# Half of the heads by 128 tokens, scores a pair ahead, loads behind points of TensorE's work

## The chip, the cores and the metric

The kernel runs on one core of a Trainium2 chip. The metric is device time in microseconds (us) of one execution; the median of several runs is given. Engines: PE is TensorE (matmul), PEld its weight loads, DVE is VectorE, ACT is ScalarE, POOL is GpSimd, SP the queue that issues all loads and stores here.

## The reference

The first part is attention with exponential decay, by blocks of 64 tokens. Shapes: q, k, v (4 batches, 8 heads, 768 tokens, 64 channels), float32, one decay `lam` for each head.

```python
for b in range(nb):                       # 12 blocks of 64 tokens
    intra = (qb @ kb.T) * Dmask           # Dmask[i, j] = lam**(i - j) for i >= j, else 0
    out_b = intra @ vb + (qb * lam**(pos + 1)) @ kv_state
    kv_state = lam**64 * kv_state + (kb * lam**(63 - pos)).T @ vb
```

The block length is a matter of arithmetic only: a state carried by 128 tokens, with a mask of 128 x 128, gives the same output. Then `x` (3072 tokens, 512 features) goes through a soft mixture of 8 experts with 4 slots each:

```python
logits = x @ phi                                  # (3072, 32)
d = softmax over tokens (axis 0); c = softmax over the 32 slots (axis 1)
slot_input = d.T @ x                              # 32 slots x 512
slot_out = relu(slot_input @ w1[e]) @ w2[e]       # w1, w2: 2 MB for each expert
y = c @ slot_out                                  # (3072, 512)
```

## The kernel before

Heads are taken in pairs: 64 channels of one head on partitions 0 to 63, of the other on 64 to 127, so there are four head pairs (`hp`), and `hh` is the half. Tokens come in chunks of 128. `PAIR[p]` takes the same chunk of two batches (index `x`); twelve pairs `p` run through the attention loop. On `s` runs the half of a chunk, 64 tokens.

One pass of the loop `for p in range(NP)`, in order on TensorE: `scores` (64x64 products of k and q into banks w0, w1; VectorE multiplies by the decay mask into `at`), `turn_k` (transposes of k; VectorE scales into `kd`), `turn_x` (transposes of the chunk finished a pass ago; ScalarE copies into `x`), `logits` in even passes or `slots` in odd ones for the group of two pairs before, `values` for the products of the other half-head's rows, `state` (kd with v, for both halves of 64 tokens), `values` again, and `carried` (the state with q scaled by `scale_q` on GpSimd) for both halves. `advance` takes the state from one half to the next: VectorE adds, GpSimd multiplies by lam**64. `evict` copies the result from four banks to `xt` on ScalarE. The two rounds of `values` differ in whether the row half and the bank half agree; the second waits for a small ScalarE copy behind the first (`behind`, `token`). Odd passes also run the softmax over slots of one group (`slot_softmax`).

Each engine keeps the order in which the program is written (`InOrder`). A float32 matmul call shows as two matmul records and two weight loads in the trace, a transpose as one of each.

All loads go through SP, in program order. At the top of pass p it has q, k, v of pair p + 2 (512 KB each, two buffers each) and up to four slabs of w1 (512 KB each, 32 slabs in all): `EARLY[p]` says how many. SP sends off whatever has a free buffer, so a load waits only for the reader of its buffer.

After the loop (the tail): the last group's logits and weights, the slot inputs, layer one (`first`, w1), layer two (`second`, w2, loaded into freed buffers: six of q, k, v, three of the work tiles, then slabs as layer one frees them), the softmax over slots transposed and stacked (`parts`, `CR`, `CT`), and the output product and stores (`put`), two chunks at a time.

Of the kernel before, what the change touches and what calls it, by code (L numbers as in the profile page):

```python
# [8 lines left out]
F32 = mybir.dt.float32  # L9
# [24 lines left out]
EARLY = (4, 3, 3, 3, 3, 3, 3, 3, 3, 3)  # L34
# [17 lines left out]
def decay_attn_soft_moe(  # L52
# [40 lines left out]
    def load_in(p, which):  # L93
        for x in which:
            tl = loads.tile([P, 2, 512], F32, tag=x, name=x)
            b, n = PAIR[p]
            src = {"q": qT, "k": kT, "v": vN}[x].rearrange("(b n) p c -> n p b c", n=NB)
            sp.dma_start(out=tl, in_=src[n, :, b:b + 2])
            IN[x, p] = tl

# [11 lines left out]
    def load_early(n):  # L112
        for _ in range(n):
            Q, kc, q = early.pop()
            t_ = slabs.tile([P, 2, 512], F32, tag="slab", name="w1t")
            sp.dma_start(out=t_, in_=w1[4 * Q + q, kc])
            wt["w1", Q, q, kc] = t_

    def load_late(pool_=None, tag="slab", bufs=None):
# [3 lines left out]
        sp.dma_start(out=t_, in_=w2[4 * Q + 2 * i:4 * Q + 2 * i + 2, f].rearrange("e p d -> p e d"))  # L123
        for y in range(2):
            wt["w2", Q, 2 * i + y, f] = t_[:, y, :]

# [10 lines left out]
    load_early(1)  # L137
# [4 lines left out]
    wps = bank("s0")  # L142
# [12 lines left out]
    mask = work.tile([P, 2, HP, C], F32, tag="mask", name="mask")  # L155
    for hh in range(2):
        for hp in range(HP):
            y = hh * HP + hp
            dve.tensor_tensor_scan(
                out=mask[:, hh, hp, :],  # L160
                data0=lam_sb[:, y:y + 1].broadcast_to([P, C]),
                data1=ident2,
                initial=0.0,
                op0=ALU.mult,
                op1=ALU.add,
            )
    kpow = mask.rearrange("p a b i -> p b a i")[:, :, :, C - 1:C].broadcast_to([P, HP, 2, DH])

    qpow = work.tile([P, HP, C], F32, tag="qpow", name="qpow")
    lam64 = qpow.rearrange("p (o a) i -> p o a i", o=1)[:, :, :, C - 1:C].broadcast_to([P, 2, HP, DH])  # L170

    def powers():
        for hp in range(HP):
            dve.tensor_tensor_scan(
                out=qpow[:, hp, :],
                data0=lam_sb[:, 8 + hp:9 + hp].broadcast_to([P, C]),
                data1=zero.broadcast_to([P, C]),
# [3 lines left out]
            )  # L181

    CN = const.tile([P, T, SL], F32, name="CN")
    acc = const.tile([P, D], F32, name="acc")
    lsum = const.tile([P, 1], F32, name="lsum")
    e = const.tile([P, P], F32, name="e")
    d = const.tile([P, P], F32, name="d")
    L = const.tile([P, P], F32, name="L")


    AT, KD, QS, ST, DEC, XT, X = {}, {}, {}, {}, {}, {}, {}
    run = {}

    def scores(p):
        k_, q_ = (IN[x, p].rearrange("p x (a s i) -> p x a s i", a=HP, s=2) for x in "kq")
        sc = [bank("w0"), bank("w1")]
        for x in range(2):
            for hp in range(HP):
                c = slice(x * 256 + hp * C, x * 256 + hp * C + C)
                for s in range(2):  # L200
                    for hh in range(2):
                        r = slice(C * hh, C * hh + C)
                        pe.matmul(
                            out=sc[hh][C * s:C * s + C, c],
                            lhsT=k_[r, x, hp, s],
                            rhs=q_[r, x, hp, s],
# [3 lines left out]
        at = work.tile([P, 2, 2, HP * C], F32, tag="at", name="at")  # L210
        for hh in range(2):
            m = mask[:, hh].rearrange("p (o a) i -> p o (a i)", o=1).broadcast_to([P, 2, HP * C])
            dve.tensor_tensor(out=at[:, hh], in0=sc[hh].rearrange("p (x c) -> p x c", x=2), in1=m, op=ALU.mult)
        AT[p] = at.rearrange("p b x (a i) -> p b x a i", a=HP)

    def scale_q(p):
        n = PAIR[p][1]
        qs = work.tile([P, 2, HP, 2, C], F32, tag="qs", name="qs")
        for x in range(2):
            q_ = IN["q", p][:, x].rearrange("p (a s i) -> p a s i", a=HP, s=2)  # L220
            s = slice(0 if n else 1, 2)
            m = qpow.rearrange("p a (o i) -> p a o i", o=1).broadcast_to([P, HP, 2, C])
            pool.tensor_tensor(out=qs[:, x, :, s], in0=q_[:, :, s], in1=m[:, :, s], op=ALU.mult)
        QS[p] = qs

    def turn_k(p):
        kd = work.tile([P, 2, HP, 2, DH], F32, tag="kd", name="kd")
        for x in range(2):
            tk = bank(f"t{x}")
            for hp in range(HP):  # L230
                c = slice(hp * P, hp * P + P)
                pe.transpose(tk[:, c], IN["k", p][:, x, c], ident)
            dve.tensor_tensor(
                out=kd[:, x], in0=tk.rearrange("p (a b c) -> p a b c", a=HP, b=2), in1=kpow, op=ALU.mult
            )
        KD[p] = kd

    def turn_x(p, tags):
        for x in range(2):
            t = chunk(p, x)  # L240
            tr = bank(tags[x])
            for y in range(HP):
                pe.transpose(tr[:, y * P:y * P + P], XT[t][:, y, :], ident)
            xn = keep.tile([P, D], F32, tag="x", name="x", bufs=6)
            act.copy(out=xn, in_=tr)
            X[t] = xn

    KV = {}

    def state(p):  # L250
        halves = (0, 1) if PAIR[p][1] < NB - 1 else (0,)
        kv = [bank(f"s{s}") for s in halves]
        v_, kd = IN["v", p].rearrange("p x (h c) -> p x h c", h=H), KD.pop(p)
        for x in range(2):
            for hp in range(HP):
                c = slice(x * 256 + hp * C, x * 256 + hp * C + C)
                for hh in range(2):
                    for s in halves:
                        r = slice(C * s, C * s + C)
                        pe.matmul(  # L260
                            out=kv[s][C * hh:C * hh + C, c],
                            lhsT=kd[r, x, hp, hh],
                            rhs=v_[r, x, HP * hh + hp],
                            start=True,
                            stop=True,
                        )
        for s in halves:
            KV[p, s] = kv[s].rearrange("p (x a c) -> p x a c", x=2, a=HP)

    def advance(p, s):  # L270

        if (p, s) not in KV:
            return
        kv = KV.pop((p, s))
        st = work.tile([P, 2, HP, DH], F32, tag="st", name="st", bufs=2)
        if PAIR[p][1] == 0 and s == 0:
            dve.tensor_copy(out=st, in_=kv)
        else:
            dve.tensor_tensor(out=st, in0=DEC.pop("d"), in1=kv, op=ALU.add)
        ST[p, s] = st  # L280
        if s == 0 and PAIR[p][1] == NB - 1:
            return
        dec = work.tile([P, 2, HP, DH], F32, tag="dec", name="dec")
        pool.tensor_tensor(out=dec, in0=st, in1=lam64, op=ALU.mult)
        DEC["d"] = dec

    def place(xb, x, hh, hp, s):
        g, a = divmod(hp, 2)
        return xb[x][hh][C * a:C * a + C, g * P + C * s:g * P + C * s + C]

    token = head.tile([P, 1], F32, name="token")

    def behind(ins, earlier):
        how = mybir.DependencyInfo(mybir.DependencyClass.Sync, mybir.DependencyReason.DATA)
        tc.add_manual_dep(ins.ins, earlier.ins.name, how, reason="row tiles change banks")
        return ins

    def values(p, xb, same):
        v_, at = IN["v", p].rearrange("p x (h c) -> p x h c", h=H), AT[p]
        for x in range(2):  # L300
            for g in range(2):
                for a in range(2):
                    for s in range(2):
                        hh, hp = s if same else 1 - s, 2 * g + a
                        r = slice(C * s, C * s + C)
                        mm = pe.matmul(
                            out=place(xb, x, hh, hp, s),
                            lhsT=v_[r, x, HP * hh + hp],
                            rhs=at[r, hh, x, hp],
                            start=(not same and g == 0),  # L310
                            stop=True,
                            skip_group_check=True,
                        )
                        if same and x + g + a + s == 0:
                            behind(mm, run["crossed"])
        if not same:

            run["crossed"] = behind(act.copy(out=token, in_=zero), mm)

    def carried(p, s, xb):  # L320
# [430 lines left out]
```

## Time and profile before

| What | Value |
|---|---|
| median of three runs | 205.86 us (205.21 to 208.71) |
| the profiled execution | 207.05 us, span 205.3 us |
| attention, first scores to last logits | 5.87 to 147.61 us |
| tail, to the end of the span | 57.66 us |
| granted TensorE clock, mean over the span | 0.902 |
| moved by DMA | 59.35 MB, mean 289 GB/s |
| loads and stores of 512 KB (256 KB for the output) | 100 (24) |

Span is from the first to the last instruction of the profiled execution; some time lies around it. A busy TensorE isn't TensorE at its peak, since matmuls overlap and their ends are modelled: the work of a group is better read from the distance between starts. "Issue" as a releaser means that an engine waited for nothing that the profile shows. Granted clock 1.00 is 2.4 GHz, 0.50 is 1.2 GHz.

### The profile page before, as it was taken

To read this page: it belongs to the slowest core of one execution; us is meant where nothing else is said; L and a number is where in the kernel's file an instruction comes from. 1 tells how busy PE (TensorE), PEld (TensorE's weight loads), DVE (VectorE), ACT (ScalarE), POOL (GpSimd) and SP (SyncE) were. 2 spreads that over 40 slices of the span, in tenths; PEclk is the share of its full clock that TensorE was granted. 3 is DMA by queue.
4 is the path that set the end of the run, shared out by engine and by line. 5 is a ranking of instruction groups with operands and counts; after the bars stand their busy time and mean duration, and the time that the engine had idled before them with its cause. 6 is when DMAs were issued, how large, how long until landed. Compare 5 with 4: busy or idle time off the path is not lost. (4 is left out here: it accounts for less than half of the span.)

```text
span 205.3 us, 8546 instructions
## 1 busy us (share of the span) xinstructions
PE 149.8 (73%) x3850; PEld 113.6 (55%) x3850; DVE 95.4 (46%) x198; ACT 56.9 (28%) x162; POOL 57.0 (28%) x72
## 2 busy tenths in 40 slices
PE   7496398397575997398295974768969999998800
PEld 7385297376565795387284854656833335444700
DVE  2835143063851663553535443755510779543800
ACT  2013022124023232224022122233320179441700
POOL 1236260262622420442602612444000049000000
PEclk9969958789996799979759699999999999999995
DMA  6999976479887299788759298445677999999996
GB/s 196 372 397 413 410 284 228 187 220 346 260 321 300 44 316 381 295 214 328 286 163 374 82 306 313 161 154 174 162 286 266 364 374 407 404 408 387 383 384 214
DMA packets 30389, 59.35 MB, mean 289 GB/s; under 512 B 2704, under 2 KB 8848, under 8 KB 30352
## 3 DMA queue, kind: packets, MB, share of 16 engines
q1 hardware_dynamic: 30352, 58.80, 80.5%
q8 instruction: 30, 0.49, 0.9%
q14 instruction: 7, 0.06, 0.1%
HBM read 52.50 MB, written 6.29 MB: 286 GB/s over the span
## 5 line engine op out<-in xcount | busy, mean ns | idle before, releaser
L46 POOL TENSOR_TENSOR dec<-st,qpow 128x512 f32<-128x512 f32 x20 | 21.2, 1059 | 75.5 <-DVE st L46 75.5
L46 DVE TENSOR_TENSOR st<-dec,s 128x512 f32<-128x512 f32 x20 | 13.7, 686 | 46.5 <-PE s L46 28.9
L46 POOL TENSOR_TENSOR qs<-q,qpow 128x512 f32<-128x512 f32 (+1 forms) x24 | 28.1, 1192 | 14.7 <-DVE qpow L46 7.9
L46 PE MATMUL t<-at,v 64*64 64x64 f32 x768 | 19.6, 231 | 15.2 <-issue 8.6
L46 PE MATMUL t<-qs,st 64*64 64x64 f32 x704 | 18.0, 247 | 14.3 <-issue 14.3
L46 PEld LDWEIGHTS t<-at,v 64*64 64x64 f32 x768 | 15.6, 141 | 22.2 <-issue 10.0
L46 PE MATMUL w<-q,k 64*64 64x64 f32 x768 | 19.2, 254 | 8.7 <-issue 7.2
L46 PEld LDWEIGHTS t<-qs,st 64*64 64x64 f32 x704 | 15.8, 158 | 15.5 <-issue 15.2
L46 ACT COPY xt<-t 128x256 f32<-128x256 f32 x48 | 14.5, 387 | 33.8 <-PE t L46 33.8
L46 DVE TENSOR_TENSOR at<-w,mask 128x512 f32<-128x512 f32 x24 | 15.4, 685 | 16.5 <-PE w L46 16.4
L46 PEld LDWEIGHTS w<-q,k 64*64 64x64 f32 x768 | 17.5, 167 | 9.8 <-issue 8.5
L46 ACT COPY x<-t 128x512 f32<-128x512 f32 x24 | 12.9, 584 | 20.6 <-PE t L46 20.6
L46 PE MATMUL w<-w2t,hz 128*32 128x256 f32 (+1 forms) x224 | 17.2, 414 | 0.9 <-DMA w2t<-w_x 0.9
L46 PE MATMUL t<-ident,k 128*128 128x128 f32 x96 | 16.5, 328 | 0.0
L46 DVE TENSOR_TENSOR kd<-t,mask 128x512 f32<-128x512 f32 x24 | 15.7, 683 | 0.8 <-PE t L46 0.7
L46 PE MATMUL t<-w1t,e 128*32 128x512 f32 x128 | 14.1, 594 | 0.4 <-DVE e L46 0.4
L46 PEld LDWEIGHTS t<-ident,k 128*128 128x128 f32 x96 | 14.0, 173 | 0.6
L46 PE MATMUL t<-ident,xt 128*128 128x128 f32 x96 | 14.0, 294 | 0.0
L46 PE MATMUL s<-v,kd 64*64 64x64 f32 x704 | 13.8, 221 | 0.0
L46 PEld LDWEIGHTS s<-v,kd 64*64 64x64 f32 x704 | 12.7, 138 | 0.0
L46 PEld LDWEIGHTS t<-ident,xt 128*128 128x128 f32 x96 | 12.5, 156 | 0.2 <-issue 0.2
L46 PEld LDWEIGHTS w<-w2t,hz 128*32 128x32 f32 x224 | 6.7, 109 | 9.3 <-issue 3.7
(105 smaller groups left out, 157.8 us busy)
## 6 DMA issues: line engine op xcount, KB each, us to landing
w1t<-w_x SPq DMA_DIRECT2D x32, 512.0 KB, 6.8
w2t<-w_x SPq DMA_DIRECT2D x32, 512.0 KB, 6.8
k<-kT SPq DMA_DIRECT2D x12, 512.0 KB, 3.8
q<-qT SPq DMA_DIRECT2D x12, 512.0 KB, 5.2
v<-vN SPq DMA_DIRECT2D x12, 512.0 KB, 6.2
y<-o SPq DMA_DIRECT2D x24, 256.0 KB, 5.4
phi_sb<-phi_x SPq DMA_DIRECT2D x4, 16.0 KB, 7.6
lam_sb<-lam_x SPq DMA_DIRECT2D x1, 6.0 KB, 3.3
```

The source lines that it names most:

```text
L46: return self._tc.keep_in_program_order(f(*args, **kwargs))
```

## The change

Head pairs 0 and 1 (`FULL`) now work by 128 tokens: mask, scores and values of 128 x 128, one state step a chunk. Head pairs 2 and 3 (`HALF`) keep blocks of 64. Scores, kd and scaled q of pair p + 1 are made during pass p. `turn_x` of pair p stands in pass p itself, and logits or slots at the end of a pass. The banks are shared out anew (xb: two instead of four). The softmax over slots leaves the loop: the logits of all groups are kept (`L` for each group), and one piece of code in the tail does them in two parts of 16 and 8 blocks of 32 columns. Output rows go by groups of pairs. `EARLY` goes; every load of the loop is held behind a matmul (`next_load`, `next_weights`), by a semaphore that SP waits for. The first head scans and the small copies for `kpow` and `qpow` change with the masks. The core of the diff:

```diff
+FULL, HALF = (0, 1), (2, 3)
...
-    load_early(1)
+    load_early(2)
...
+    def scores_half(p):
+        k_, q_ = kq(p)
         for x in range(2):
+            for i, hp in enumerate(HALF):
                 for s in range(2):
+                    t = slice(C * s, C * s + C)
                     for hh in range(2):
                         pe.matmul(
+                            out=ub[hh][rows(s), x * P + i * C:x * P + i * C + C],
+                            lhsT=k_[rows(hh), x, hp, t],
+                            rhs=q_[rows(hh), x, hp, t],
...
+    def scores_full(p):
...
+        for x in range(2):
+            for i, hp in enumerate(FULL):
+                for hh in range(2):
+                    mm = pe.matmul(
+                        out=wb[hh][:, (2 * x + i) * P:(2 * x + i) * P + P],
+                        lhsT=k_[rows(hh), x, hp],
+                        rhs=q_[rows(hh), x, hp],
...
+    def values_full(p):
...
         for x in range(2):
+            for hh in range(2):
+                for i, hp in enumerate(FULL):
+                    mm = pe.matmul(
+                        out=xb[hh][rows(i), x * 256:x * 256 + P],
+                        lhsT=v_[:, x, HP * hh + hp],
+                        rhs=at_f[:, hh, x, P * i:P * i + P],
...
+    def carried_full(p):
...
+                    mm = pe.matmul(
+                        out=xb[hh][rows(i), x * 256:x * 256 + P],
+                        lhsT=st[rows(hh), x, hp],
+                        rhs=qs[rows(hh), x, hp],
...
+    def state_full(p):
...
+                    pe.matmul(
+                        out=sb[rows(hh), c:c + C],
+                        lhsT=kd[:, x, hp, hh],
+                        rhs=v_[:, x, HP * hh + hp],
...
+    def step(out, dec, kv, fresh):
+        if fresh:
+            dve.tensor_copy(out=out, in_=kv)
+        else:
+            dve.tensor_tensor(out=out, in0=dec, in1=kv, op=ALU.add)
...
+    def next_load(p, which, at):
+        if p + 2 < NP:
+            behind(load_in(p + 2, which), at)
+        else:
+            behind(load_late(loads, which, 2), at)
+
+    def next_weights(at):
+        if early:
+            behind(load_early(1), at)
+
+    turn_k(0, 0, xb[0])
+    scores_half(0)
+    scores_full(0)
+    turn_k(0, 1, xb[1])
+    masked(at_h, ub, mask_h, 2 * C)
+    masked(at_f, wb, mask_f, 2 * P)
+    powers()
+    scale_q(0)
     for p in range(NP):
...
+        top, mm = values_half(p, False)
+        crossed = behind(act.copy(out=token, in_=zero), mm)
+        next_load(p, "k", top)
+        state_half(p, 0)
+        if g is not None and even:
+            new = highest(g)
+        step(mid, dec_h, kv_half(0), n == 0)
+        if more:
+            scores_half(p + 1)
+        if not last:
+            state_half(p, 1)
+            pool.tensor_tensor(out=dec_m, in0=mid, in1=lam_h, op=ALU.mult)
+        if g is not None and even:
+            weigh(g, new)
+        mm, _ = values_half(p, True)
+        behind(mm, crossed)
+        next_weights(mm)
+        if n > 0:
+            carried_full(p)
+            carried_half(p, 0, st[:, :, 2:4])
+        carried_half(p, 1, mid)
+        if not last:
+            step(st[:, :, 2:4], dec_m, kv_half(1), False)
+        if g is not None and not even:
+            gather(g)
+        if more:
+            masked(at_h, ub, mask_h, 2 * C)
+        mm = values_full(p)
+        next_load(p, "q", mm)
+        if not last:
+            state_full(p)
+            step(st[:, :, 0:2], dec_f, sb[:, 0:256].rearrange("p (x a c) -> p x a c", x=2, a=2), n == 0)
+            pool.tensor_tensor(out=dec_h, in0=st[:, :, 2:4], in1=lam_h, op=ALU.mult)
+            pool.tensor_tensor(out=dec_f, in0=st[:, :, 0:2], in1=lam_f, op=ALU.mult)
...
+            act.copy(
+                out=XT[p][:, :, 2 * hh:2 * hh + 2],
...
+        mm = None
+        if more:
+            scale_q(p + 1)
+            mm = scores_full(p + 1)
+            masked(at_f, wb, mask_f, 2 * P)
+        if g is not None and even:
+            turn_e()
+        if more:
+            turn_k(p + 1, 0, tb)
+        mm2 = turn_x(p, 0)
+        next_load(p, "v", mm or mm2)
+        next_weights(mm2)
+        if more:
+            turn_k(p + 1, 1, wb[0])
+        turn_x(p, 1)
+        if even:
+            mm = slots(g) if g is not None else None
+        else:
+            mm = logits((p - 1) // 2)
+        if mm is not None and p % 3:
+            next_weights(mm)
...
-    for _ in slot_softmax(G - 1, lpb[:, 0:P]):
-        pass
+    CN = slabs.tile([P, T, SL], F32, tag="slab", name="CN")
+    for k, lp in ((slice(0, 16), lt[0]), (slice(16, T), lt[1][:, 0:256])):
...
+        dve.tensor_reduce(out=c, in_=lv, axis=AX.X, op=ALU.max)
+        dve.tensor_tensor(out=CN[:, k], in0=lv, in1=c_, op=ALU.subtract)
+        act.activation(out=CN[:, k], in_=CN[:, k], func=AF.Exp)
+        dve.tensor_reduce(out=c, in_=CN[:, k], axis=AX.X, op=ALU.add)
+        dve.tensor_scalar(out=c, in0=c, scalar1=1e-9, scalar2=None, op0=ALU.add)
+        dve.reciprocal(out=c, in_=c)
+        pool.tensor_tensor(out=CN[:, k], in0=CN[:, k], in1=c_, op=ALU.mult)
```

## Rows read from the trace of the kernel before

**Rows 1.** Windows: stretch, its us, busy us by engine, clock, DMA share, GB/s.

```profile
63.80:69.50 5.70, 5.64 (x121) 5.52 (x121) 2.69 (x5) 1.47 (x5) 3.52 (x3) 0.50 0.37 146
130.00:147.00 17.00, 13.27 (x496) 10.92 (x500) 9.72 (x21) 5.21 (x19) 5.29 (x5) 1.00 0.53 172
5.87:147.61 141.74, 101.84 (x3370) 88.77 (x3370) 67.44 (x129) 34.59 (x111) 49.16 (x45) 0.88 0.76 268
149.65:205.27 55.62, 42.88 (x451) 20.02 (x451) 25.19 (x57) 19.32 (x45) 7.12 (x20) 0.95 0.96 352
```

**Rows 2.** Waits of TensorE, whole span: waiting <- releaser: us, times, longest.

```profile
PE t L46 <- issue: 22.9, 9, 4.0
PE w L46 <- issue: 8.6, 4, 3.8
PE t L46 <- DVE kd L46: 3.7, 3, 2.3
PE t L46 <- ACT x L46: 2.9, 5, 0.9
```

**Rows 3.** Timeline of TensorE: start, us, operation, records [idle before it <- releaser].

```profile
10.37 0.69 PE L46 MATMUL t<-at,v 64*64 64x64 f32 x32 [2.29 <-DVE kd L46]
...
49.45 1.27 PE L46 MATMUL t<-qs,st 64*64 64x64 f32 x64
50.67 0.33 PE L46 MATMUL w<-q,k 64*64 64x64 f32 x4
53.73 1.15 PE L46 MATMUL w<-q,k 64*64 64x64 f32 x60 [2.73 <-issue]
54.81 1.09 PE L46 MATMUL t<-ident,k 128*128 128x128 f32 x8
...
56.70 1.08 PE L46 MATMUL w<-xt,phi_sb 128*32 128x128 f32 x32
57.72 0.69 PE L46 MATMUL t<-at,v 64*64 64x64 f32 x32
58.23 1.11 PE L46 MATMUL s<-v,kd 64*64 64x64 f32 x64
59.16 0.65 PE L46 MATMUL t<-at,v 64*64 64x64 f32 x32
...
63.86 1.44 PE L46 MATMUL t<-qs,st 64*64 64x64 f32 x43 [3.72 <-issue]
...
134.19 0.51 PE L46 MATMUL t<-at,v 64*64 64x64 f32 x20 [0.35 <-issue]
```

**Rows 4.** Part 3 of the page: the code queue; packets, MB, engines' share.

```profile
q8 instruction: 30, 0.49, 0.9%
```

**Rows 5.** Part 1 of the page: busy time and records of each engine.

```profile
PE 149.8 (73%) x3850; PEld 113.6 (55%) x3850; DVE 95.4 (46%) x198; ACT 56.9 (28%) x162; POOL 57.0 (28%) x72
```

**Rows 6.** The DMA view from 61.5 to 62.6 us; columns as in rows 4.

```profile
q1 hardware_dynamic: 113, 0.43, 97.3%
q8 instruction: 1, 0.02, 5.3%
```

**Rows 7.** Timeline of SP: first and last of six loads, 512 KB each.

```profile
55.93 0.38 SPq L46 DMA_DIRECT2D k<-kT  x1
...
60.30 0.47 SPq L46 DMA_DIRECT2D w1t<-w_x  x1
```

**Rows 8.** Part 5 of the page: busy, mean ns, idle before, releaser.

```profile
L46 DVE TENSOR_TENSOR kd<-t,mask 128x512 f32<-128x512 f32 x24 | 15.7, 683 | 0.8 <-PE t L46 0.7
```

**Rows 9.** Loads of q (view by tile), from issue to landing.

```profile
DMA to landing us min/median/max: 4.0/5.2/7.7
```

**Rows 10.** Timeline of VectorE in the tail.

```profile
161.80 0.25 DVE L46 TENSOR_REDUCE cmx<-s 128x4 f32<-128x128 f32 x1
...
163.88 0.98 DVE L46 STREAM_TRANSPOSE part<-CN 128x768 f32<-128x768 f32 x1
```

**Rows 11.** Loads of w1 (view by tile), from issue to landing.

```profile
DMA to landing us min/median/max: 4.9/6.8/9.1
```

More of the change, by code (lines that the diff above doesn't have):

```diff
@@ L167, in decay_attn_soft_moe @@
[L167 to L177, printed above, removed]
+    mask_f = work.tile([P, 2, 2, P], F32, tag="mask_f", name="mask_f")
@@ new lines, in decay_attn_soft_moe @@
+    mask_h = work.tile([P, 2, 2, C], F32, tag="mask_h", name="mask_h")
+    for m_, diagonal, heads in ((mask_h, ident2, HALF), (mask_f, ident, FULL)):
+        for hh in range(2):
+            for i, hp in enumerate(heads):
+                y = hh * HP + hp
+                dve.tensor_tensor_scan(
+                    out=m_[:, hh, i, :],
+                    data0=lam_sb[:, y:y + 1].broadcast_to([P, m_.shape[3]]),
+                    data1=diagonal,
+                    initial=0.0,
+                    op0=ALU.mult,
+                    op1=ALU.add,
+                )
@@ new lines, in decay_attn_soft_moe @@
+    kpow = head.tile([P, HP, 2], F32, name="kpow")
+    for m_, heads in ((mask_h, HALF), (mask_f, FULL)):
+        end = m_.shape[3]
+        pool.tensor_copy(
+            out=kpow[:, heads[0]:heads[0] + 2],
+            in_=m_.rearrange("p b a i -> p a b i")[:, :, :, end - 1:end].rearrange("p a b o -> p a (b o)"),
+        )
+    qpow = work.tile([P, HP, P], F32, tag="qpow", name="qpow")
+    qpow_ = qpow.rearrange("p (o a) i -> p o a i", o=1)
+    lam_f = qpow_[:, :, 0:2, P - 1:P].broadcast_to([P, 2, 2, DH])
@@ L178, in powers @@
+    lam_h = qpow_[:, :, 2:4, C - 1:C].broadcast_to([P, 2, 2, DH])
+    def powers():
+        for hp in HALF + FULL:
+            width = P if hp in FULL else C
+            dve.tensor_tensor_scan(
+                out=qpow[:, hp, 0:width],
+                data0=lam_sb[:, 8 + hp:9 + hp].broadcast_to([P, width]),
+                data1=zero.broadcast_to([P, width]),
                 initial=1.0,
@@ L238, in turn_x @@
-    def turn_x(p, tags):
-        for x in range(2):
[L240 to L318, printed above, removed]
@@ L320, in carried @@
-    def carried(p, s, xb):
-        if PAIR[p][1] == 0 and s == 0:
-            return
-        st = ST.pop((p, 0) if s else (p - 1, 1))
-        for x in range(2):
-            for hp in range(HP):
-                for hh in range(2):
-                    r = slice(C * hh, C * hh + C)
-                    pe.matmul(
-                        out=place(xb, x, hh, hp, s),
-                        lhsT=st[r, x, hp],
-                        rhs=QS[p][r, x, hp, s],
+            q_ = IN["q", p][:, x].rearrange("p (a i) -> p a i", a=HP)
@@ new lines, in scale_q, with turn_k @@
+            if n:
+                pool.tensor_tensor(out=qs[:, x], in0=q_, in1=qpow, op=ALU.mult)
+            else:
+                pool.tensor_tensor(out=qs[:, x, 2:4, C:P], in0=q_[:, 2:4, C:P], in1=qpow[:, 2:4, C:P], op=ALU.mult)
+    def turn_k(p, x, tk):
+        for hp in range(HP):
+            c = slice(hp * P, hp * P + P)
+            pe.transpose(tk[:, c], IN["k", p][:, x, c], ident)
+        dve.tensor_tensor(
+            out=kd[:, x],
+            in0=tk.rearrange("p (a b c) -> p a b c", a=HP, b=2),
+            in1=kpow.rearrange("p a (b o) -> p a b o", o=1).broadcast_to([P, HP, 2, DH]),
+            op=ALU.mult,
+        )
@@ new lines, in turn_x, with values_half @@
+    def turn_x(p, x):
+        tr = xb[x]
+        first = None
+        for y in range(HP):
+            mm = pe.transpose(tr[:, y * P:y * P + P], XT[p][:, x, y, :], ident)
+            first = first or mm
+        xn = keep.tile([P, D], F32, tag="x", name="x", bufs=6)
+        act.copy(out=xn, in_=tr)
+        X[p, x] = xn
+        return first
+    def values_half(p, same):
+        v_ = v_of(p)
+        first = None
+        for x in range(2):
+            for i, hp in enumerate(HALF):
+                for s in range(2):
+                    hh = s if same else 1 - s
+                    mm = pe.matmul(
+                        out=xb[hh][rows(i), x * 256 + P + C * s:x * 256 + P + C * s + C],
+                        lhsT=v_[rows(s), x, HP * hh + hp],
+                        rhs=at_h[rows(s), hh, x, C * i:C * i + C],
+                        start=(not same and x == 0),
+                        stop=True,
+                        skip_group_check=True,
+                    )
+                    first = first or mm
+        return first, mm
@@ L332, in carried @@
+    def values_full(p):
+        v_ = v_of(p)
+        first = None
+        for x in range(2):
+            for hh in range(2):
+                for i, hp in enumerate(FULL):
[3 more added lines that the diff above has]
+                        rhs=at_f[:, hh, x, P * i:P * i + P],
                         start=False,
@@ L335, in carried @@
                     )
-    def evict(p, xb):
+                    first = first or mm
+        return first
+    def carried_full(p):
+        first = None
         for x in range(2):
-            xt = keep.tile([P, HP, P], F32, tag="xt", name="xt")
-            for hh in range(2):
-                act.copy(
-                    out=xt[:, 2 * hh:2 * hh + 2], in_=xb[x][hh][:, 0:2 * P].rearrange("p (a b) -> p a b", a=2)
-                )
-            XT[chunk(p, x)] = xt
+            for i, hp in enumerate(FULL):
+                for hh in range(2):
+                    mm = pe.matmul(
+                        out=xb[hh][rows(i), x * 256:x * 256 + P],
+                        lhsT=st[rows(hh), x, hp],
+                        rhs=qs[rows(hh), x, hp],
+                        start=False,
+                        stop=True,
+                        skip_group_check=True,
+                    )
+                    first = first or mm
+        return first
@@ new lines, in carried_half @@
+    def carried_half(p, s, state):
+        for x in range(2):
+            for i, hp in enumerate(HALF):
+                for hh in range(2):
+                    pe.matmul(
+                        out=xb[hh][rows(i), x * 256 + P + C * s:x * 256 + P + C * s + C],
+                        lhsT=state[rows(hh), x, i],
+                        rhs=qs[rows(hh), x, hp, C * s:C * s + C],
+                        start=False,
+                        stop=True,
+                        skip_group_check=True,
+                    )
@@ new lines, in kv_half, with state_half @@
+    def kv_half(s):
+        return hb[s][:, 0:256].rearrange("p (x a c) -> p x a c", x=2, a=2)
+    def state_half(p, s):
+        v_ = v_of(p)
+        for x in range(2):
+            for i, hp in enumerate(HALF):
+                for hh in range(2):
+                    c = x * P + i * C
+                    pe.matmul(
+                        out=hb[s][rows(hh), c:c + C],
+                        lhsT=kd[rows(s), x, hp, hh],
+                        rhs=v_[rows(s), x, HP * hh + hp],
+                        start=True,
+                        stop=True,
+                    )
@@ L347, in decay_attn_soft_moe @@
+    token = head.tile([P, 1], F32, name="token")
     sel = const.tile([P, SL], F32, name="sel")
@@ L421, in slots, with turn_e @@
+    def turn_e():
+        dp = sb[:, 384:512]
+        pe.transpose(dp, e, ident)
+        act.copy(out=d, in_=dp)
     def slots(g):
-        psl = bank("w0")
-        for c, t in enumerate(group(g)):
-            pe.matmul(
-                out=psl[SL * c:SL * c + SL, :], lhsT=d[:, SL * c:SL * c + SL], rhs=X[t], start=True, stop=True
-            )
-        run["psl"] = psl
+        first = None
+        for c, m in enumerate(members(g)):
+            mm = pe.matmul(
+                out=wb[1][SL * c:SL * c + SL, :], lhsT=d[:, SL * c:SL * c + SL], rhs=X[m], start=True, stop=True
+            )
+            first = first or mm
+        return first
@@ L444, in decay_attn_soft_moe @@
+    powers()
+    scale_q(0)
     for p in range(NP):
[L445 removed]
+        b, n = PAIR[p]
         even = p % 2 == 0
[L447 to L457 removed]
@@ L458, in decay_attn_soft_moe @@
-        if p == 0:
-            powers()
-        scale_q(p)
-        if pend is not None and not even:
-            lp = turn_weights()
-            sm = slot_softmax(pend, lp)
-        turn_k(p)
-        if pend is not None and not even:
-            next(sm)
-        if p > 0:
-            turn_x(p - 1, ("t2", "t3"))
-        if pend is not None:
-            (logits if even else slots)(pend)
-        xb = [[bank(f"t{2 * x + hh}") for hh in range(2)] for x in range(2)]
-        values(p, xb, False)
@@ L473, in decay_attn_soft_moe @@
-        state(p)
-        advance(p, 0)
-        if pend is not None and even:
-            weigh(pend)
-        values(p, xb, True)
-        if pend is not None and not even:
-            gather(pend)
-        carried(p, 0, xb)
-        carried(p, 1, xb)
-        advance(p, 1)
-        evict(p, xb)
-        if pend is not None and not even:
-            next(sm)
+        last = n == NB - 1
+        more = p + 1 < NP
+        g = (p - 2) // 2 if p >= 2 else None
+        top, mm = values_half(p, False)
@@ new lines, in decay_attn_soft_moe @@
+        XT[p] = keep.tile([P, 2, HP, P], F32, tag="xt", name="xt", bufs=2)
+        for hh in range(2):
+            act.copy(
+                out=XT[p][:, :, 2 * hh:2 * hh + 2],
+                in_=xb[hh].rearrange("p (x a i) -> p x a i", x=2, a=2),
+            )
+        mm = None
[7 more added lines that the diff above has]
+            turn_k(p + 1, 0, tb)
@@ L494, in decay_attn_soft_moe @@
+    for tag in ("kd", "qs", "at_f"):
+        load_late(work, tag)
+    g = G - 1
     own = const.tile([P, 1], F32, name="own")
     gm = const.tile([P, 4], F32, name="gm")
-    logits(G - 1)
-    pl = run["pl"]
-    new = highest(G - 1)
-    act.copy(out=L, in_=pl)
-    turn_x(NP - 1, ("t0", "t1"))
+    new = highest(g)
+    act.copy(out=L[:, g], in_=pl)
+    lt = [bank("w1"), bank("w0")]
+    for i in range(4):
+        pe.transpose(lt[0][:, i * P:i * P + P], L[:, i], ident)
     dve.tensor_scalar(out=gm, in0=gsel, scalar1=new, scalar2=None, op0=ALU.mult)
-    lpb = bank("s0")
```

219 lines of the change are left out of this document (97 added, 122 removed).

## The prediction

> **What bounds the kernel now.** I read the stretches first [rows 1], because the kernel has two stages with different limits. From 5.87 us to the end of the last logits at 147.61 (the attention stage) TensorE is busy 101.84 of 141.74 us, VectorE 67, GpSimd 49, ScalarE 35, the DMA engines have a share of 0.76, and the granted clock averages 0.88. Nothing is full: this stage is a chain with holes. From 149.65 on, the DMA share is 0.96: the tail is set by bytes.
>
> The waits say what the holes are [rows 2]. 31.5 us in 13 pieces are "issue": TensorE waited for no semaphore that the profile shows. 6.6 us are waits for kd and for ScalarE's copy of x. The timeline of one pair of chunks [rows 3] shows the size: 2.73 us inside the scores, 3.72 us inside the carried products. They fall in the middle of a run of like matmuls, so no data are missing. What is missing is code. The DMA has a queue of its own for it, 30 packets in the run [rows 4], for 3850 matmuls and as many weight loads [rows 5], so one packet for about 257 TensorE instructions. In the 1.1 us up to 62.6 one of these packets passed, among loads that took 97% of the engines [rows 6], and 1.3 us later, at 63.86, TensorE goes on. Ahead of it stood what the SP queue had sent off from 55.93 to 60.30: six loads of 512 KB (k, q, three w1, v) in 4.4 us [rows 7], which at the tail's rate of about 400 GB/s need 7.9 us. So a code packet asked for in a dense stretch waits behind a heap of loads. The counterexample is in rows 1: from 130 to 147 us the DMA moves 172 GB/s, the clock is 1.00, and an issue gap there is 0.35 us [rows 3]. A long gap is paid twice: after 63.8 the clock is 0.50 for 5.7 us [rows 1], that is 1.2 instead of 2.4 GHz.
>
> The account of the stage: one pair at full clock, from rows 3 by the distance between starts, is scores 64 records x 18.0 ns (1.08 us for 60) = 1.15; k and x turned 1.89; logits 1.02 (slots in the other pairs taken as equal); values 64 x 16 = 1.02; state 0.93; carried 64 x 19 = 1.22; turning e and L about 0.1: 7.35 us. Twelve make 88.2, less 2.1 for pair 0, whose scores and keys lie ahead of the first value product at 10.37: 86.1. With 31.5 and 6.6 that is 124.2 of the 137.2 us from 10.37 to 147.6; the other 13 I put down to the half clock.
>
> The Trainium skill speaks against this reading: "Runtime: NRT & Kernel Launch", section "Instruction fetch mechanics", calls the cost of crossing a 16 KiB block of instructions mostly hidden. By it the 31.5 us would have another cause, and spacing the loads would leave them; the packet in rows 6 and the light stretch in rows 1 disagree with it. That is the third rival below.
>
> **The change part by part.**
>
> *Matmul calls.* In two of the four head pairs one 128-token product replaces two 64-token ones. Of scores, values, state and carried each loses 8 of 32 calls in a pair, 384 calls in all (two records each: 768 matmuls and 768 weight loads fewer, so about 6 code packets of 30). The array's time grows nevertheless. The halves keep their price: scores 0.58, values 0.51, state 0.46, carried 0.61. A full score or value record has twice the columns, and only two run at a time instead of four. From below: four times state's 14.5 ns, 58 ns x 16 = 0.93 each. From above, with no overlap: the pitch of the k and x transposes, 118 ns x 16 = 1.89. Full state 16 x 29 to 58 = 0.46 to 0.93; full carried, still quadrants with twice the columns, 16 x 38 = 0.61. I take the lower ends, since quadrants and the 32-column tiles visibly overlap in this trace (64 state records in 0.93 us) and the new calls alternate rows or columns. The pair: 0.58+0.93+0.51+0.93+0.46+0.46+0.61+0.61+1.89+1.02+0.1 = 8.1 us, 0.75 more than now. Upper end 10.5.
>
> *The order.* Scores of the next pair, its k and the state step now stand one to six products ahead of their use. kd for pair p+1 is turned before x of pair p and before logits or slots (about 2 us), so the 6.6 us of waits mostly go. I keep 0.3 a pair for what is late next: ScalarE's two copies into XT, which have state_full, scores_full and one turning (about 1.9 us) to finish in. VectorE gains two masks and one step a pair, at 0.34 to 0.68 us each (half to all of the 128x512 multiply [rows 8]), and loses the slot softmax; its 67 us in 142 leave room. GpSimd's three scalings of 128x256 replace two of 128x512. The manual wait of the same-half values on the token copy exists before as well; four groups lie between now.
>
> *The loads.* Per pair still k, q, v and 2.7 of w1, 3 MB or about 7.4 us at 400 GB/s, but each is sent when TensorE passes a point: k at the first values, w1 at the second, q at the full values, v and w1 in the turning, w1 in logits or slots. So one or two loads stand ahead of a code packet, not up to six. The gaps now cost 31.5+13 = 44.5 us, 3.7 a pair. From below a pair could cost 0 (nothing waits), from above 3.7. The light stretch is nearest, 0.35 a gap; but the DMA will be busier than there (7.4 in 9.4 us), and the dense part (values, state, next scores, carried: 144 of some 230 records in about 2.8 us) runs faster than its code may arrive. I take 1.0.
>
> SP waits at each point, and all later loads are queued behind it. Who waits for them: scores_half(p+2) for q(p+2). Between the point that releases q and that product lie full values 0.93, full state 0.46, full scores 0.93, turnings 1.9, logits 1.02, half values 0.25, state 0.23: 5.7 us, against an issue of 0.4 and a landing of 4.0 to 7.7, median 5.2 [rows 9]. Without the present heaps the lower half is nearer; no charge. But the loop has a bound: q's landing, the issue, and the 2.5 us from the scores back to the next full value product. A pair can't be shorter than landing + 3.0 us: 8.2 at the median.
>
> *Start and end.* Lead-in: kd and scores of pair 0 stand ahead of the loop as before, with four scans doubled in width; the first value product stays near 10.4. The last pair prepares no successor: 0.58+0.93+0.93 and the later states, 3.1 us off. Tail now: 205.27 - 147.61 = 57.66 us. It keeps 23 loads of w2 and 6.3 MB of output, 18.4 MB, 46 us at 400 GB/s. The first five groups' slot softmax moves here; the last group's alone took 161.80 to 163.88 [rows 10]. Six groups in two pieces, on VectorE, ScalarE and GpSimd in turn, are an estimated 6.3 us by the slope between 0.25 us (128x128, rows 10) and 0.68 (128x512, rows 8). That is 4.2 more ahead of the transposed part and of the second h, whose layer two can wait; but the DMA covers it as long as w2 loads are due, and the tail's early stretch may lose less than it does now. From -4 to +5; I take +1: 58.7.
>
> *Sum.* Pair 8.1+0.3+1.0 = 9.4. 10.4 + 12 x 9.4 - 3.1 = 120.1; plus 58.7 a span of 178.8. The profiled execution took 207.05 for its 205.30 (1.75 around it) and stands 1.2 above the median 205.86. So 178.8+1.75-1.2 = 179.3; **179 us**, own range 168 to 189 (pair 8.5 to 10.3).
>
> **Rivals.**
>
> 1. *Half of the gaps stay.* The DMA is busy four fifths of the time, and a code packet still finds two or three loads ahead: 1.9 a pair instead of 1.0, with some half clock, 10.3 to 11.1 a pair: 189 to 200 us. For it: in rows 6 the loads alone filled the engines. Chance 0.18.
> 2. *Full products don't overlap in the array.* 10.5 a pair, sparser code (0.6): 11.4 with the waits, 24 us more than forecast: 203, no change. For it: no row shows a 64x128 or 128x64 tile. Against: all smaller tiles overlap. 0.10.
> 3. *The gaps aren't the loads' doing* (the page's rule). Then 3.7 a pair stay on top of 8.1+0.3: 12.1, about 211 us, at the edge of slower. Against: rows 6 and the light stretch. 0.06.
> 4. *Slower: q comes late.* Place: scores_half of the next pair. By the bound above, a landing of 9.1 us, the longest of w1 [rows 11], makes each pair 12.1 and the whole 211. It decides from a landing of 6.4 on (the pair of 9.4), and makes the kernel slower from about 9.0 (a pair of 12.0). For it: SP sends nothing early any more. Against: q's longest now is 7.7, with heaps ahead. 0.06.
>
> That leaves 0.56 for the forecast and 0.04 for less than 168 (pairs at TensorE's own pace, a shorter tail).
>
> **Numbers.** A measurement of this kernel can tell about 2% from no change: 201.7 to 210. Faster: 0.56+0.18+0.04 = 0.78. Rival 2 and half of rival 3 are within: 0.13. Slower: 0.06+0.03 = 0.09. The range goes from 168 to 203: it leaves out 0.04 below and 0.12 above with rivals 3 and 4, and some of the upper edge.
>
> **What would show it.** Right: issue waits of TensorE under 15 us instead of 31.5, clock above 0.95 in the attention stage, logits ending near 120, some 24 code packets, full scores at about 58 ns a record. Wrong: 118 ns a record there (rival 2); issue gaps of 3 us beside a DMA that is not full (rival 3); TensorE waiting for a q or k load (rival 4); a tail over 62 us, with layer two waiting for hz.

## The result, and the profile after

The changed kernel takes 186.78 us (median of 4 runs, 184.76 to 188.22); the kernel before 207.29 in the same comparison. The ratio is 0.9055, with a 95% interval of 0.8906 to 0.9203: faster. The forecast of 179 us was 4% too low, inside its range of 168 to 203. Further down, the profiles of before_spaced, tail_order, dense_diluted and hz_between are of runs 2 to 4% longer than the fastest of their kernel, so the sizes of their waits are less sure; the times given are medians of all runs, and the ratios leave such longer runs out.

The two stages first, by windows (stretch, its length, busy us of PE, PEld, DVE, ACT, POOL, then clock, DMA share, GB/s); these answer to [rows 1].

```profile
5.45:125.20 119.75, 105.24 (x2607) 91.23 (x2606) 60.75 (x137) 34.03 (x85) 46.18 (x58) 0.97 0.91 309
125.20:184.60 59.40, 44.46 (x463) 21.20 (x459) 28.42 (x65) 20.69 (x48) 8.78 (x22) 0.92 1.00 356
150.00:155.00 5.00, 1.53 (x24) 0.97 (x28) 4.83 (x10) 4.87 (x12) 4.49 (x12) 0.93 1.05 387
```

The last logits end at 125.2 instead of 147.6 us: 22.4 us gained. TensorE's busy time rose by 3.4 us, with fewer records (2607 for 3370): the stage is shorter because its holes are, 14.5 us without a matmul instead of 39.9. The tail went from 57.7 to 59.4. The third line is a stretch in it in which TensorE mostly stands still and the DMA does not.

The waits of TensorE (us in total, times, longest), to be held against [rows 2]:

```profile
PE a L46 <- issue: 9.0, 6, 2.3
PE w L46 <- DVE hz L46: 4.0, 1, 4.0
...
PE u L46 <- DMA q<-qT: 1.2, 2, 1.0
PE w L46 <- issue: 0.9, 3, 0.3
```

Issue waits are 10.1 us in all (with 0.2 in a line not shown) instead of 31.5, the longest 2.3 instead of 4.0. The page has the instructions and the code packets [rows 4, 5]:

```profile
PE 153.7 (83%) x3082; PEld 116.4 (63%) x3082; DVE 90.4 (49%) x206; ACT 56.0 (30%) x134; POOL 55.7 (30%) x87
...
q8 instruction: 24, 0.39, 0.9%
```

Parts of three passes on TensorE's timeline (start, us, operation, records), as [rows 3]:

```profile
23.50 1.09 PE L46 MATMUL a<-at_f,v 128*64 128x128 f32 x16
24.42 0.63 PE L46 MATMUL s<-v,kd 128*64 128x64 f32 x16
24.99 1.16 PE L46 MATMUL w<-q,k 64*128 64x128 f32 x16
26.08 0.65 PE L46 MATMUL r<-ident,k 128*128 128x128 f32 x4
...
27.97 1.08 PE L46 MATMUL s<-xt,phi_sb 128*32 128x128 f32 x32
28.98 0.46 PE L46 MATMUL a<-at_h,v 64*64 64x64 f32 x16
...
33.70 0.40 PE L46 MATMUL a<-qs,st 64*64 64x64 f32 x13 [2.25 <-issue]
...
41.49 0.46 PE L46 MATMUL a<-at_h,v 64*64 64x64 f32 x16
...
43.17 0.27 PE L46 MATMUL a<-qs,st 64*64 64x128 f32 x1
...
44.34 0.65 PE L46 MATMUL a<-at_f,v 128*64 128x128 f32 x6
46.78 0.76 PE L46 MATMUL a<-at_f,v 128*64 128x128 f32 x9 [1.78 <-issue]
```

From the distances: full values 0.92, full state 0.57, full scores 1.09, turnings 1.89, logits 1.01; the five groups of 64-token records ahead of the carried products 1.68 (41.49 to 43.17), carried 1.17. With 0.08 for turning e that is 8.4 us a pair. The two gaps stand where the dense stretch ends: in the carried products and just behind them. (The dense stretch is what follows logits or slots in a pass: values, state, next scores and carried, 144 short records with nothing longer between.)

What the issue waits are can be counted in the traces. Number TensorE's instructions from the start: matmuls, weight loads and the few that handle semaphores. All 107 issue waits of the eleven profiles of this document end at a number that leaves 193 or 194 when divided by 256, about what one code packet holds, and 1.1 to 1.6 us after a packet of the code queue landed. Up to the last logits, each packet starts between 0.2 us before and 4.6 us after TensorE passes the preceding number of this kind, never earlier: code comes only about one packet ahead. For the packets that ended a wait, the median of that delay is 3.6 us in the kernel before and 2.8 in the changed one.

### The profile page after: what moved, and what is told of

Read it like the earlier page. It is cut to its first block, busy times and chain, and to the rows that moved or that the text cites. A ratio compares the mean times of both kernels' runs of the same rounds, so it can differ in the third digit from the quotient of the medians.

```text
span 184.6 us, 7075 instructions
## 1 busy us (share of the span) xinstructions
PE 153.7 (83%) x3082; PEld 116.4 (63%) x3082; DVE 90.4 (49%) x206; ACT 56.0 (30%) x134; POOL 55.7 (30%) x87
## 5 line engine op out<-in xcount | busy, mean ns | idle before, releaser
L46 ACT COPY xt<-a 128x512 f32<-128x512 f32 x24 | 12.9, 589 | 44.2 <-PE a L46 44.2
L46 PE MATMUL w<-w2t,hz 128*32 128x256 f32 (+1 forms) x224 | 17.5, 450 | 4.0 <-DVE hz L46 4.0
L46 DVE TENSOR_TENSOR at_f<-w,mask_f 128x512 f32<-128x512 f32 x24 | 15.5, 686 | 10.0 <-PE w L46 10.0
L46 ACT COPY x<-a 128x512 f32<-128x512 f32 x24 | 14.0, 587 | 19.3 <-PE a L46 19.3
L46 PE MATMUL a<-at_f,v 128*64 128x128 f32 x192 | 14.7, 291 | 3.4 <-issue 3.4
L46 PE MATMUL w<-q,k 64*128 64x128 f32 x192 | 16.3, 308 | 0.6 <-issue 0.6
L46 PE MATMUL a<-ident,xt 128*128 128x128 f32 x96 | 14.5, 274 | 0.5 <-ACT xt L46 0.5
L46 PEld LDWEIGHTS w<-q,k 64*128 64x128 f32 x192 | 13.6, 210 | 2.0 <-issue 1.1
L46 PE MATMUL a<-at_h,v 64*64 64x64 f32 x384 | 12.6, 227 | 2.1 <-DVE at_h L46 1.4
L46 PEld LDWEIGHTS a<-at_f,v 128*64 128x64 f32 x192 | 11.0, 141 | 4.7 <-issue 3.9
L46 PEld LDWEIGHTS a<-ident,xt 128*128 128x128 f32 x96 | 11.1, 140 | 1.0 <-ACT xt L46 1.0
```

The source lines that it names most:

```text
L46: return self._tc.keep_in_program_order(f(*args, **kwargs))
```

## The experiments

Two theories stood against each other. A: TensorE's issue gaps are code packets that come late because loads stand ahead of them, so spacing the loads is what counts. B: the new order and the fewer instructions give the gain by themselves. Ratios are to the kernel before, run beside it on the same chip.

**no_spacing** puts the loads of the changed kernel back at the top of a pass.

```diff
+        if p + 2 < NP:
+            load_in(p + 2, "kq")
+        if early:
+            load_early(1)
+        if p + 2 < NP:
+            load_in(p + 2, "v")
+        if early:
+            load_early(min(1 + (p % 3 > 0), len(early)))
...
-        next_load(p, "k", top)
-        next_weights(mm)
-        next_load(p, "q", mm)
```

> The changed kernel with its loads put back at the top of a pass (k, q, one w1, v, one or two w1, each held only by its buffer). Theory A (code packets stand behind heaps of loads, and spacing the loads is what shrinks TensorE's issue gaps): the issue waits rise from 10 us to 20-30 us, stretches at half clock come back, logits end at 133-142 us instead of 125, and the kernel takes 194-202 us. Theory B (the new order and the fewer instructions give the gain, the spacing nothing): 185-188 us with issue waits of 10-12 us.

Measured: 203.54 us, ratio 0.9808 (0.9709 to 0.9908); logits end at 142.9. Its waits:

```profile
PE a L46 <- issue: 14.6, 5, 3.4
PE w L46 <- issue: 4.9, 2, 2.6
...
PE s L46 <- issue: 2.8, 1, 2.8
```

22.3 us of gaps and seven spells at half clock ahead of the tail, against two. The delay of the code packets that ended a wait has a median of 3.9 us. A is borne out, 1.5 us above its range: by the ratios (0.9055 and 0.9808), four fifths of the gain are gone without spacing.

**before_spaced** spaces the loads of the kernel before, and nothing else.

```diff
-        scores(p)
+        mm = scores(p)
+        if p:
+            next_weights(mm)
...
-        turn_k(p)
+        next_load(p, "k", turn_k(p))
...
+        next_load(p, "q", values(p, xb, False))
+        mm = state(p)
+        if p % 3:
+            next_weights(mm)
+        next_weights(values(p, xb, True))
+        next_load(p, "v", carried(p, 1, xb))
```

> The kernel before with nothing changed but its loads: each held behind a matmul (w1 behind the scores, k behind its transposes, q behind the first values, w1 behind state in two passes of three, w1 behind the second values, v behind the carried products). Theory A: issue waits fall from 31.5 us to 14-20 us, the whole to 191-198 us. Theory B: 204-208 us, issue waits as before.

Measured: 195.36 us, ratio 0.94 (0.9292 to 0.9509); logits end at 138.0.

```profile
PE t L46 <- issue: 17.2, 8, 3.9
PE w L46 <- issue: 8.1, 5, 3.3
```

The time is as A had it, the reason only half: in its profile the gaps fell by 6.2 us, not by the 11.5 to 17.5 expected, and the spells at half clock ahead of the tail came to 27.3 us instead of 34.1. How large the gaps are in a typical run of it isn't shown. Spacing alone is worth 6%, order and 128 tokens alone 2%; their product, 0.922, lies just above the upper edge of the change's interval (0.9203), and both factors have intervals of about 0.01 either way, so whether the two strengthen each other isn't shown.

**before_w1_late** takes the loads of w1 out of the kernel before's loop; all 31 go behind it.

```diff
-EARLY = (4, 3, 3, 3, 3, 3, 3, 3, 3, 3)
+EARLY = ()
...
+    load_early(len(early))
     for x in "kqv":
```

> The kernel before with all but one load of w1 taken out of the attention loop and put behind it, so that the DMA is lightly loaded there. Theory A: issue waits of TensorE in the attention stage under 8 us, clock near 1.00, the last logits end at 108-120 us instead of 147.6; the whole gets longer, 205-225 us, since 16 MB move into the tail. Rival (the gaps are not the loads' doing, the page's rule that code loading is hidden): issue waits stay near 30 us and logits end near 147 us.

Measured: 214.2 us (one run); logits end at 125.8, with a clock of 0.96 and 201 GB/s in the stage.

```profile
PE t L46 <- issue: 14.3, 9, 2.6
...
PE w L46 <- issue: 3.0, 4, 1.6
```

The rival (gaps that loads don't cause) is refuted: the logits end 22 us earlier, and 14 us of the gaps go. But my bound failed as well: 17.3 us of gaps are left (0.4 of it in the tail), where I said under 8. Loads ahead make the gaps long (the longest falls from 4.0 to 2.6); they aren't the only cause. A code packet needs some time even on a lighter loaded DMA: at the gaps here it started 1.8 us (median) after TensorE had passed the preceding such number, took 0.9 us or more, and TensorE went on 1.3 to 1.6 us after its landing. The code of one packet is 128 matmuls with their weight loads, and 128 short records take 2.0 to 2.4 us (16 to 19 ns each by [rows 3]).

**all_half** runs all head pairs by 64 tokens, in the changed kernel's order, with spaced loads.

```diff
-FULL, HALF = (0, 1), (2, 3)
+FULL, HALF = (), (0, 1, 2, 3)
...
-        next_weights(mm)
+        next_load(p, "q", mm)
         if n > 0:
-            carried_full(p)
-            carried_half(p, 0, st[:, :, 2:4])
-        carried_half(p, 1, mid)
+            carried_half(p, 0, st)
+        mm = carried_half(p, 1, mid)
...
+        next_weights(mm)
```

> The changed kernel with all four head pairs by 64 tokens (no 128-token products), same order, loads still spaced (q at the second values, w1 behind the carried products). The array's time of a pair falls from 8.35 to about 7.5 us, the code packets rise from 24 to 30, and values, state, next scores and carried become one dense stretch of 256 records, two packets' worth, in about 4.3 us. Theory A (code arrival bounds the pair): issue waits 22-35 us, logits end at 128-140 us, 190-202 us in all: the 128-token half of the change pays through fewer instructions although it costs array time. Rival (array time rules): logits end at 115-119 us, 177-181 us in all.

Measured: 208.03 us, ratio 0.9952 (0.9882 to 1.0023); logits end at 143.6.

```profile
PE a L46 <- issue: 13.1, 6, 3.4
PE u L46 <- issue: 7.7, 3, 3.4
PE w L46 <- issue: 5.2, 3, 3.2
```

26.0 us of gaps: A on the gaps, and slower than either range. The order by itself, with loads spaced nearly alike, loses to before_spaced: it puts values, state, next scores and carried into one stretch of 256 short records. Only together with the 128-token products does it pay; they thin that stretch to 144 and bring the code packets from 30 to 24, and this run doesn't tell which of the two counts. So the 128 tokens are worth about 9% here (0.9952 to 0.9055), although they add to the array's time.

**after_w1_late** takes the loads of w1 out of the changed kernel's loop (`next_weights` does nothing); they go behind it.

```diff
     def next_weights(at):
-        if early:
+        if False:
```

> The changed kernel with all but two loads of w1 taken out of the attention loop and put behind it (k, q, v keep their points). If what is left of the issue gaps (10 us in the changed kernel) is loads standing ahead of code, they fall under 3 us. If it is mostly the code packet's own way, which a dense stretch is too short for, they stay at 6-10 us. Logits end at 121-125 us either way; the whole gets longer, 200-220 us, since 16 MB move into the tail.

Measured: 213.95 us (one run); logits end at 117.2. Windows and waits:

```profile
5.45:117.20 111.75, 100.39 (x2604) 87.10 (x2602) 60.62 (x136) 33.98 (x85) 46.14 (x58) 1.00 0.67 196
```

```profile
PE a L46 <- issue: 5.5, 5, 1.3
...
PE w L46 <- issue: 1.8, 3, 1.3
```

7.5 us of gaps (with 0.2 in a line not shown) with a quieter DMA, none over 1.3: most of the changed kernel's 10.1 us stay, as the second reading had it (q, k and v still load here, so not all of it need be the packet's own way). Logits end 4 us earlier than I said: the loads of w1 cost the stage 8.0 us, of which the gaps explain 2.6. With them go the two spells at half clock, 6.8 us long and so worth 3.4 at most; the other 2 us I can't place.

**dense_diluted** moves values_full up between state_half(0) and scores_half, and state_full ahead of the second values: the same instructions, the short ones less close together.

```diff
+        at = values_full(p)
+        next_load(p, "q", at)
         if more:
             scores_half(p + 1)
         if not last:
             state_half(p, 1)
...
+        if not last:
+            state_full(p)
         mm, _ = values_half(p, True)
```

> The changed kernel with values_full moved up between state_half(0) and scores_half, and state_full between state_half(1) and the second values: the same instructions, but the dense stretch of 64-token records is diluted with 32 long ones (q's load goes out with values_full, so earlier). Theory A (code arrives at its own pace, and the gaps fall at the end of the dense stretch): issue waits fall from 10 us to 4-7 us, logits end at 119-123 us instead of 125; the whole takes 181-185 us, or less of a gain if the DMA (share 0.91 in this stage) takes part of it back. Rival (what is left of the gaps is heaps of loads, not density): issue waits stay at 9-11 us, 186-188 us.

Measured: 186.33 us, ratio 0.896 (0.8895 to 0.9024); logits end at 126.1. Not told apart from the change. Its timeline and its waits:

```profile
49.87 0.46 PE L46 MATMUL a<-at_h,v 64*64 64x64 f32 x16
50.15 0.64 PE L46 MATMUL r<-v,kd 64*64 64x64 f32 x16
50.72 1.09 PE L46 MATMUL a<-at_f,v 128*64 128x128 f32 x16
51.74 0.69 PE L46 MATMUL u<-q,k 64*64 64x64 f32 x32
52.26 0.64 PE L46 MATMUL w<-v,kd 64*64 64x64 f32 x16
52.83 0.69 PE L46 MATMUL s<-v,kd 128*64 128x64 f32 x16
53.45 0.46 PE L46 MATMUL a<-at_h,v 64*64 64x64 f32 x16
```

```profile
PE a L46 <- issue: 4.1, 4, 1.5
...
PE w L46 <- DVE st L46: 2.6, 7, 0.4
...
PE s L46 <- issue: 1.5, 1, 1.5
...
PE w L46 <- issue: 1.4, 1, 1.4
```

The gaps fell to 7.0 us, as A had it, and the stage ran at full clock throughout; the time, and the logits' end, are not A's but lie in the rival's range or beyond. The fall is more than profiles of one loop differ by: three of the change's loop (the change, tail_order, hz_between) have 10.1, 8.4 and 12.2 us, two of this one (dense_diluted, both_orders) 7.0 and 4.8. That density did it isn't shown, for q's load goes out earlier as well. What was won went into the array: the five 64-token groups now take 0.28+0.57+0.52+0.57+0.28 = 2.22 us instead of 1.68, 0.54 a pair, since each state group, now with a full product next behind it, takes 0.57 instead of about 0.3; and VectorE's st is waited for seven times.

**tail_order** asks whether the softmax that moved into the tail costs what TensorE waits for hz (4.0 us). T1: no, bytes set the tail's end. T2: yes.

```diff
     for _ in range(4):
         load_late()
+    first(1)
     CN = slabs.tile([P, T, SL], F32, tag="slab", name="CN")
...
     stack((act.copy, pool.tensor_copy, dve.tensor_copy))
-    first(1)
```

> The changed kernel with layer one's second half (first(1)) placed ahead of the softmax over slots, so that VectorE and ScalarE finish h and hz of it before that softmax. TensorE's wait of 4.0 us for hz and the half clock after it should go under either theory. Theory T1 (the tail is set by bytes: the DMA share there is 1.00): the time stays within 1 us of the changed kernel's (186 to 188). Theory T2 (the moved softmax costs the tail what TensorE waits): 181-183 us.

Measured: 192.31 us, ratio 0.9258 (0.92 to 0.9316): slower than the change, which neither theory had (the intervals just touch; both_orders below repeats it). Waits, and a window:

```profile
PE w L46 <- DVE CN L46: 6.1, 1, 6.1
```

```profile
165.00:170.00 5.00, 5.00 (x23) 1.91 (x23) 0.43 (x1) 0.96 (x2) 0.00 (x0) 0.50 0.15 57
```

Layer two writes bank w0, where the logits of the softmax lie: the wait for hz became one for CN, 6.1 us. The stacked parts, and with them the first store, came at 169.4 instead of 162.6, when the last loads had landed: the DMA fell to a share of 0.15.

**both_orders** joins the two reorderings, the edits of dense_diluted and tail_order as they stand above.

> Both reorderings together. T1 with A: like dense_diluted alone, 181-185 us. T2 with A: 176-180 us.

Measured: 192.84 us, ratio 0.9291 (0.9226 to 0.9356), with the same wait of 6.1 us for CN. It missed for the same reason.

**hz_between** puts first(1) behind the softmax and the transpose of its result, ahead of CR and the stacks: no bank in the way.

```diff
     dve.transpose(out=parts[1], in_=CN)
+    first(1)
     act.copy(out=parts[0].bitcast(F32R), in_=parts[1])
...
-    first(1)
```

> The changed kernel with layer one's second half placed after the softmax over slots and the transpose of its result, but ahead of the copies into CR and CT. Bank w0, which held up tail_order, is read to its end as early as in the changed kernel; h and hz come about 4 us earlier, the stacked parts about 2 us later. TensorE's 4.0 us for hz should shrink to under 1 us and the half clock after it go. T1 (bytes set the tail's end, since its loads and stores keep the DMA busy without a hole): 185.5-188 us. T2 (the wait for hz costs what it lasts): 181-184 us.

Measured: 188.11 us, ratio 0.905 (0.897 to 0.913), the change's own. The wait for hz is gone and another stands there:

```profile
PE u L46 <- ACT so L46: 3.4, 1, 3.4
```

ScalarE was still casting the stacked parts when `so` was due. T1 holds as far as this goes: in the changed kernel the DMA's share is 0.98 or more from 135 to 180 us, and SP sends the 24 stores one right behind the other, so that TensorE's wait ahead of them seems free.

```profile
162.59 18.49 SPq L46 DMA_DIRECT2D y<-o  x24
```

That a wait as long stood elsewhere in hz_between keeps it from being a clean proof. tail_order supports it from the other side: there the hole appeared, and the time rose.

## Why the prediction was right, and where its terms were off

*The mechanism* held in its direction: gaps of code behind heaps of loads were the largest item, and shortening them is most of the gain. The waits are for code, as the count by 256 shows, and the packets start late behind loads, as their delay shows: a median of 3.6 us at the gaps before and 3.9 in no_spacing, 2.8 in the change, 1.8 and 1.6 where w1 is out of the loop. Issue waits under 15 us (10.1), clock above 0.95 in the stage (0.97), 24 code packets: as said. Logits ended at 125.2, not near 120; the terms below say why.

*The array's price* was 8.1 us a pair and came out at 8.41. Full scores and values do overlap (rival 2 is out: 68 and 58 ns a record, not 118), but scores at 68 and full state at 36 ns lie above my lower ends of 58 and 29 (0.16 and 0.11 us a pair), and the five 64-token groups took 1.68 instead of 1.55; carried gave 0.05 back. 0.31 x 12 = 3.7 us. (The pair of the kernel before adds up to 7.33 by its terms, where I wrote 7.35.)

*Gaps and half clock* were put at 1.0 a pair: measured 10.1 us, and about 3.6 left for the clock after the pairs' 12 x 8.41 and 2.8 us of other waits are taken from the 117.4 us (10.88 to 125.2, plus the forecast's 3.1 for what the last pair saves, not measured): 1.1 a pair. The two spells at half clock in the stage, 6.8 us, can make up 3.4 of it at most. But the reason given for the size was half wrong, and that the size came out is in part luck. I took the light stretch's 0.35 us as what is left without loads ahead; before_w1_late and after_w1_late leave 17.3 and 7.5 us. What the change gains on the gaps comes from spacing (no_spacing takes it away) and from the 128-token products (all_half takes them away). These bring fewer instructions and a dense stretch of 144 instead of 256 records, which no run here separates.

*Waits for data* at 0.3 a pair: 2.8 us behind the first value product, 0.23. q, whose lateness was rival 4, cost 1.2 us, 0.2 of it ahead of the loop; its landing is 4.2 to 7.4 us, median 5.2, about as before [rows 9].

*Start and end*: the first value product at 10.88 instead of 10.4; the tail 59.4 instead of 58.7, with layer two waiting for hz as feared and at no cost that hz_between could show.

*The sum*: 3.7 (array) + 0.9 (gaps, clock and waits) + 0.5 (start) + 0.7 (tail) = 5.8 us, which is the span's 184.6 less the forecast's 178.8. The term that was mis-sized is the array's: I took the lower end for all new shapes, which was right for the full values; full scores lay a sixth above it, full state a quarter.

*Rival 3*, that the gaps aren't the loads' doing, is refuted for about half of them: in before_w1_late 14 of 31.5 us go with the loads of w1, and the stage ends 22 us earlier. The Trainium skill ("Runtime: NRT & Kernel Launch", section "Instruction fetch mechanics") calls the cost of crossing a 16 KiB block of instructions mostly hidden. The traces disagree with it: TensorE lost 31.5 us at such crossings in the kernel before, and 7.5 us in after_w1_late.

## What to carry to other kernels

Here short matmul records used up code faster than it arrived, and loads queued ahead of a code packet made that worse: count TensorE instructions per microsecond along the order, not only its busy time, and hold big loads behind points of the work instead of sending what has a buffer. An order that hides data waits can lose more than it gains if it packs the short records together (all_half against before_spaced). Where the DMA ran without a hole to the end, a wait of TensorE in that stretch seemed free (hz_between), but delaying the first store past the last load was not (tail_order).

## What the runs showed of the hardware that I had not expected

With the DMA at 196 to 201 GB/s in the attention stage TensorE still lost 7.5 us (after_w1_late) and 17.3 us (before_w1_late) to issue gaps. Every issue wait fell on a multiple of 256 instructions (shifted by 193 or 194), and code came only about one packet ahead. Tiles of unlike shape next to each other cost: a 64x64 state group of 16 records took 0.57 us with a full product next behind it (dense_diluted) and about 0.3 among its like. Records of 64x128 ran at 68 ns, of 128x64 with the same number of columns at 58.
